# Attention and an MLP on one core: q and k stored with tokens inside, v by two pairs of heads, and the small sums one row block later

## The chip, the cores and the metric

The kernel runs on one core of a Trainium2 chip. Its engines work side by side, each on a queue of its own: TensorE multiplies matrices (PE in the profile, PEld for its weight loads), VectorE (DVE) and ScalarE (ACT) work element by element, GpSimd (POOL) adds a little, and SyncE (SP) does nothing but issue DMAs. All DMAs that SP issues stand in one queue and are issued in order. The metric is the device time of one launch in microseconds. What numpy does to the inputs ahead of the launch is not in it.

## The reference

Sigmoid attention with 8 batches, 12 heads, 448 tokens and 64 dimensions a head, and behind it an MLP over all 3,584 tokens (768 to 2,048 to 768). The weights come in 64-bit floats, the rest in 32-bit.

```python
def _attn_ref(q, k, v):                     # each (8, 12, 448, 64)
    scale = 1.0 / np.sqrt(q.shape[-1])
    scores = scale * np.matmul(q, k.transpose(0, 1, 3, 2)) - np.log(S)
    attn = 1.0 / (1.0 + np.exp(-scores))
    return np.matmul(attn, v)

def _moe_ref(x, w_in, w_out):               # x (3584, 768), w_in (768, 2048), w_out (2048, 768)
    h = x @ w_in
    g = h - np.tanh(h)
    return g @ w_out
```

## The kernel before, in words

The program goes through the batches. A batch has attention over six pairs of heads (a pair fills the 128 partitions with 2 x 64 dimensions), then a first product `moe1` (x times w_in, line 763), the function g on VectorE and ScalarE (`mix`, `halves`), and a second product `moe2` (g times w_out, lines 878 and 916). While TensorE runs `moe2` of one batch, the attention of the next is woven in step by step.

*Precision.* From batch 1 on, every 32-bit operand is scaled by a power of two and split in a high and a low float16 half, and a product takes three float16 matmuls. The scale comes from a sum of squares: `norm` squares a tile on ScalarE and adds it up (line 317), `scales` adds over the partitions by a matmul with ones (`pbn`, line 325), reads that on ScalarE (`tn`, line 327) and makes the scale from it in six small VectorE operations (`un`, `n_y`, `in`, `sn`, `rn`). These are the small sums. Batch 0 is multiplied in 32-bit and needs none.

*Layout.* A score matmul needs the 64 dimensions of a head on the partitions, but q and k lie in memory with tokens outside and dimensions inside, 256 bytes a row. `load_qk` loads a pair into `kn` and `qn`, [112 tokens, 4, 2 heads, 64]. In batch 0 `prep` turns them on TensorE (`transpose`, lines 309 and 641: into PSUM as `KT`, `QT`, then a copy to `KS` on VectorE and to `QS` on ScalarE). Later `parts` splits them in two halves `w`, and a transposing DMA on SP's queue (line 356) turns `w` into `K` and `Q`. `load_v` loads v in two to four DMAs a pair; the last 64 tokens of two pairs share a tile.

*Weights.* During batch 0's attention the 64-bit w_in is loaded in 24 pieces (`raw`, line 131, five buffers) and each is cut to 32 bits: `sta` on ScalarE (line 146), three operations on VectorE (151, 152, 155), a square (`sq`, 167 or 169) and a sum `cn`. w_out follows in 32 pieces (`rawo`, `stb`, sums `wl`). The first product of batch 0 runs in 32-bit on the cut w_in; w_in and w_out are split in halves (216, 219) in batch 0's second product.

*The order of the work.* On PE, ACT, DVE and POOL the program is issued as it is written; SP's queue is ordered by a planner in batch 0 and by the program from batch 1 on. The attention of batches 1 to 7 is a generator `stream`. For two pairs g and h = g + 1 it yields five steps: A, scores of g's first two key blocks, and products with v left over from before; B, the other scores of g, and the squares of k and q of g + 3; S, `scales(g + 2)` and the split of K of g + 2; C, scores of h, products with v, splits of Q and v of g + 2; D, the last scores of h, splits of K and Q of g + 3. When each step is issued is a table of numbers: `BLOCKS` (and `BLOCKS1` in batch 1) counts the row blocks of `moe2`, one for each of the 16 blocks of w_out's rows and each of three tiles of 128 tokens, six matmuls a block; the rest of 64 tokens counts half. In `BLOCKS` the entries are D, A, B, S, C, D, A, B, S, C, D, A, B, S, C, so S stood two blocks ahead of C: at 18, 34 and 50. Three more events at a batch's end (`batch_scales`, at the 12th entry plus 3, 5 and 7, thus at 46, 48 and 50) scale and split x for the next first product.

Of the kernel before, what the change touches and what calls it, by code (L numbers as in the profile page):

```python
# [8 lines left out]
F16 = mybir.dt.float16  # L9
BF16 = mybir.dt.bfloat16  # L10
F32 = mybir.dt.float32
# [3 lines left out]
AF = mybir.ActivationFunctionType  # L15
ALU = mybir.AluOpType
# [3 lines left out]
P = 128  # L20
D = 64
CK = 112
QT = 3
# [11 lines left out]
class Builder:  # L35
# [7 lines left out]
    BLOCKS = (8, 11, 16, 18, 20, 24, 27, 32, 34, 36, 40, 43, 48, 50, 52)  # L43
# [3 lines left out]
    BLOCKS1 = (4, 6, 7, 10, 13, 16, 18, 20, 24, 27, 32, 34, 36, 40, 43, 48, 50, 52)  # L47
# [5 lines left out]
    def __init__(self, ctx, tc, q, k, v, w_in, w_out, out):  # L53
        self.tc, self.nc = tc, tc.nc
        self.q, self.k, self.v, self.w_in, self.w_out, self.out = q, k, v, w_in, w_out, out
        self.B, self.H, self.S, _ = q.shape
        self.DM, self.DFF = w_in.shape
        self.NP = self.H // 2
# [3 lines left out]
        nc = self.nc  # L62
# [217 lines left out]
    def load_qk(self, b, j):  # L280

        out = []
        for name, src in (("kn", self.k), ("qn", self.q)):
            t = self.nat.tile([CK, 4, 2, D], F32, name=name)
            for h in range(2):
                queue = self.nc.scalar if name == "qn" and b + j == 0 else self.nc.sync
                queue.dma_start(t[:, :, h, :], src[b, 2 * j + h].rearrange("(c p) d -> p c d", c=4))
            out.append(t)
        return out

    def load_v(self, b, j, pool, tag, bufs):


        n = 2 * QT + (0 if j % 2 else 2)
        t = pool.tile([P, n, D], F32, name="vn", tag=tag, bufs=bufs)
        dma = self.nc.sync.dma_start
        for h in range(2):
            dma(t[:, h * QT : (h + 1) * QT], self.v[b, 2 * j + h, : QT * P].rearrange("(c p) d -> p c d", c=QT))
# [6 lines left out]
    def transpose(self, n, name, tag="tr", bufs=1):  # L305
        nc = self.nc
        t = self.ps.tile([P, 512], F32, name=name, tag=tag, bufs=bufs)
        for c in range(4):
            nc.tensor.transpose(t[:, c * CK : (c + 1) * CK], n[:, c].rearrange("p h d -> p (h d)"), self.ident[:CK, :CK])
        return t[:, : self.S]  # L310

    def norm(self, t, out):

        flat = t.rearrange("p a b d -> p (a b d)" if len(t.shape) == 4 else "p a d -> p (a d)")
        rows, n = flat.shape
        junk = self.sm.tile([P, 8 * D], BF16, name="sqn", tag="sq", bufs=2)
        self.nc.scalar.activation(junk[:rows, :n], flat, AF.Square, accum_out=out[:rows])  # L317
# [27 lines left out]
    def parts(self, n, s, name, act):  # L345

        nc = self.nc
        flat = n.rearrange("p c h d -> p (c h d)")
        w = self.qk.tile([CK, 2, 4 * P], F16, name="w", tag="w", bufs=2)
        if act:  # L350
            nc.scalar.activation(w[:, 0], flat, AF.Copy, scale=s[:CK])
        else:
            nc.vector.tensor_scalar(w[:, 0], flat, s[:CK], None, op0=ALU.mult)
        nc.vector.scalar_tensor_tensor(w[:, 1], flat, s[:CK], w[:, 0], op0=ALU.mult, op1=ALU.subtract)
        o = self.qk.tile([P, 2, self.S], F16, name=name, tag=name)
        nc.sync.dma_start_transpose(
            o.rearrange("p x (c t) -> p (x c) t", c=4), w.rearrange("p x e -> p (x e)")
        )
        return o
# [257 lines left out]
    def attention32(self, b, weights, rest):  # L617
# [5 lines left out]
        load = lambda j: self.load_qk(b, j) + [self.load_v(b, j, self.att, "vhl", 3)]  # L623
# [8 lines left out]

        def prep(j):
            out = []
            for n, name in ((0, "K"), (1, "Q")):
                t = self.transpose(loaded[j][n], name + "T", *((), ("mm", 2))[n])
                o = self.qk.tile([P, S], F32, name=name + "S", tag=name)
                if n:
                    nc.scalar.activation(o, t, AF.Copy)
                else:  # L640
                    nc.vector.tensor_copy(o, t)
                out.append(o[:, None])
            return out
# [17 lines left out]
        self.warm(14)  # L661
        qk = {0: prep(0)}
        self.warm(4)
        order = [(j, c) for j in range(NP) for c in (range(QT) if j % 2 else range(QT + 1))]
        for n, (j, c) in enumerate(order):
            both = (j, j + 1) if c == QT else (j,)
            ps = self.scores([qk[i][0] for i in both], [qk[i][1] for i in both], c)
# [5 lines left out]
            if c == (1, 0)[j % 2] and j + 1 < NP:  # L673
                qk[j + 1] = prep(j + 1)
# [398 lines left out]
```

## Time and profile before

| | us |
|---|---|
| median of 3 runs | 1241.29 (1240.48 to 1241.41) |
| the profiled execution, own time | 1240.89 |
| its span | 1239.1 |
| PE busy | 1182.8 (95%) |
| DVE busy | 927.8 (75%) |
| ACT busy | 887.6 (72%) |
| POOL busy | 77.7 (6%) |
| loads of k and q | 96 and 96 DMAs of 112 KB |
| loads of v | 96 DMAs of 96 KB, 48 of 32 KB |
| transposing DMAs | 42 for K, 42 for Q |
| DMA packets under 512 bytes | 213,936 of 225,679 |

A stage has its own bound, and the shares above are averages over all stages. A timeline row reads: start, length, engine, line, operation, output and inputs, and in brackets the idle time ahead of it with what ended it. A row of waits reads: who waited, for whom, microseconds in total, how often, the longest. A row of a group of instructions reads: count, then busy time in total and the mean in ns of one, then the idle time ahead of the group. SPq stands for the issue of a DMA on SP's queue.

### The profile page before, as it was taken

The numbers are of one execution on the slowest core, as the hardware profiler recorded it, in microseconds if no ns is written. First come the engines' busy times: TensorE is split into PE (matmuls) and PEld (weight loads), VectorE is DVE, ScalarE is ACT, GpSimd is POOL, SyncE is SP. The second block draws the span as 40 slices with busy tenths as digits, with TensorE's granted clock in tenths as the row PEclk, the third lists the DMA queues.
The fourth block names the chain that finished last, engine by engine and source line by source line (L and its number), as shares of the span: only waits on it lengthen the run. The fifth ranks groups of instructions, "written<-read, shape, count | busy, mean of one in ns | idle before, by whom it ended". The sixth has DMA issues, their size and how long they took to land.

```text
span 1239.1 us, 19719 instructions
## 1 busy us (share of the span) xinstructions
PE 1182.8 (95%) x7633; PEld 606.5 (49%) x7633; DVE 927.8 (75%) x1376; ACT 887.6 (72%) x1238; POOL 77.7 (6%) x62
## 2 busy tenths in 40 slices
PE   8889867899999999999999999999999999999998
PEld 3235423455445555555555555455554555455555
DVE  5899967788976789667976789667976789636930
ACT  5767776877887678876887678875887768754820
POOL 0100000000002000200002000110001000110000
PEclk9999988899999999999999999999999999999999
DMA  9973358230045400542014410442014510300000
GB/s 228 264 206 91 83 115 213 56 75 7 1 88 116 94 17 1 114 92 65 1 44 102 91 35 1 100 106 65 1 43 88 96 44 1 65 22 20 2 13 33
DMA packets 225679, 89.78 MB, mean 72 GB/s; under 512 B 213936, under 2 KB 215728, under 8 KB 225584
## 3 DMA queue, kind: packets, MB, share of 16 engines
q1 hardware_dynamic: 224656, 88.28, 30.6%
q8 instruction: 60, 0.98, 0.3%
q10 hardware_dynamic: 928, 0.23, 0.1%
q14 instruction: 35, 0.29, 0.1%
HBM read 58.20 MB, written 11.01 MB: 56 GB/s over the span
## 4 chain that ended last, share of the span: by engine, by line
PE 77%; DVE 8%; ACT 8%; issue 3%; DMA 3%; SPq 1%; ACTq 0%; DVEq 0%
PE ph L763 30%; PE po L878 27%; PE acc L411 8%; PE sc L380 7%; PE por L916 4%; ACT a L391 3%; ACT sqn L317 2%; DMA raw<-moe_w_in 1%; DMA qn<-q 1%; DVE m L837 1%; DVE m L848 1%; DVE sta L152 1%; DVE m L851 1%; DVE m L844 1%; DVE g L748 1%
## 5 line engine op out<-in xcount | busy, mean ns | idle before, releaser
L878 PE MATMUL po<-wo,g 128*128 128x384 f16 x2304 | 397.4, 328 | 6.2 <-ACT wo L216 3.1
L763 PE MATMUL ph<-xhl,wi 128*128 128x448 f16 x2016 | 382.6, 352 | 0.0
L878 PEld LDWEIGHTS <-g 128*128 128x128 f16 x2304 | 220.2, 99 | 176.5 <-issue 38.4
L763 PEld LDWEIGHTS <-wi 128*128 128x128 f16 x2016 | 196.7, 98 | 185.0 <-issue 1.8
L398 DVE SCALAR_TENSOR_TENSOR ahl<-a,ahl 128x896 f16<-128x896 f32 x126 | 156.6, 1277 | 140.9 <-ACT ahl L397 140.5
L391 ACT ACTIVATE a<-sc,nls,rn 128x896 f32<-128x896 f32 x147 | 156.1, 1088 | 61.9 <-PE sc L380 59.0
L833 ACT ACTIVATE u<-ph,ih 128x896 f32<-128x896 f32 x64 | 64.4, 1006 | 94.3 <-PE ph L763 89.7
L397 ACT ACTIVATE ahl<-a 128x896 f16<-128x896 f32 x126 | 113.1, 940 | 0.6
L380 PE MATMUL sc<-Q,K 64*128 64x448 f16 x1008 | 106.3, 368 | 4.7 <-ACT a L391 2.5
L837 DVE SCALAR_TENSOR_TENSOR m<-ph,ihk,u 128x896 f32<-128x896 f32 x64 | 73.6, 1150 | 35.0 <-ACT th L835 34.6
L747 ACT ACTIVATE g<-m,Sg 128x896 f16<-128x896 f32 x64 | 66.6, 1041 | 34.4 <-DVE m L851 29.1
L851 DVE COPY_PREDICATED m<-u,th 128x896 f32<-128x896 uint32 x64 | 77.4, 1210 | 6.6
L411 PE MATMUL acc<-ahl,vhl 128*64 128x448 f16 (+1 forms) x864 | 81.0, 357 | 0.0
L748 DVE SCALAR_TENSOR_TENSOR g<-m,Sg,g 128x896 f16<-128x896 f32 x64 | 73.5, 1148 | 8.1 <-ACT g L747 8.1
L848 DVE SCALAR_TENSOR_TENSOR m<-q,m 128x896 f32<-128x896 f32 x64 | 69.9, 1092 | 10.9 <-ACT q L847 3.8
L793 PE MATMUL ph<-x,wi 128*128 128x448 f32 x192 | 75.1, 540 | 0.2 <-DVE x L423 0.2
L838 DVE SCALAR_TENSOR_TENSOR th<-ph,ih,th 128x896 f32<-128x896 f32 x64 | 73.3, 1146 | 0.0
L850 ACT ACTIVATE u<-u,b 128x896 f32<-128x896 f32 x64 | 66.7, 1043 | 7.2 <-DVE m L837 5.2
L439 POOL TENSOR_TENSOR x<-x 128x448 f32<-128x448 f32 x24 | 22.4, 932 | 786.3 <-ACT x L427 786.3
L380 PEld LDWEIGHTS <-K 64*128 64x128 f16 x1008 | 36.7, 99 | 68.9 <-issue 45.6
L844 DVE SCALAR_TENSOR_TENSOR m<-q,m 128x896 f32<-128x896 f32 x64 | 69.6, 1088 | 0.0
L916 PE MATMUL por<-wo,g 128*64 128x384 f16 x768 | 65.8, 327 | 1.1 <-ACT o L907 1.1
(133 smaller groups left out, 1195.0 us busy)
## 6 DMA issues: line engine op xcount, KB each, us to landing
raw<-moe_w_in SPq DMA_DIRECT2D x24, 512.0 KB, 5.2
rawo<-moe_w_out SPq DMA_DIRECT2D x32, 384.0 KB, 4.4
kn<-k SPq DMA_DIRECT2D x96, 112.0 KB, 3.0
qn<-q SPq DMA_DIRECT2D x94, 112.0 KB, 3.1
vn<-v SPq DMA_DIRECT2D x96, 96.0 KB, 2.9
out<-o SPq DMA_DIRECT2D x21, 384.0 KB, 2.4
vn<-v SPq DMA_DIRECT2D x48, 32.0 KB, 2.4
out<-orem SPq DMA_DIRECT2D x16, 96.0 KB, 2.2
```

What stands on the lines that cost most here:

```text
L380: self.nc.tensor.matmul(ps[i * m : (i + 1) * m, h, : self.S], K[i][r, w, c * P : c * P + m], Q[i][r, x, :], start=(n == 0), stop=(n == len ...
L391: self.nc.scalar.activation(a[:, 0], ps[:, :, : self.S], AF.Sigmoid, bias=self.nls, scale=scale)
L397: nc.scalar.activation(A[:, 0], a[:, 0], AF.Copy, scale=A_SCALE)
L398: nc.vector.scalar_tensor_tensor(A[:, 1], a[:, 0], A_SCALE, A[:, 0], op0=ALU.mult, op1=ALU.subtract)
L411: self.nc.tensor.matmul(acc[i][h * D : (h + 1) * D, : self.S], v[k, w, 2 * QT + h if half else h * QT + c], A[k, x, h], start=(n == 0 and ...
L748: nc.vector.scalar_tensor_tensor(g[:, 1], m, Sg, g[:, 0], op0=ALU.mult, op1=ALU.subtract)
L763: nc.tensor.matmul(ph[:, e, :S], self.wi[:, c * self.NB + k, part, e * P : (e + 1) * P], xhl[c][:, x, :], start=(i == 0), stop=(i == 3 * s ...
L837: V.scalar_tensor_tensor(m, ps, ihk, u, op0=ALU.mult, op1=ALU.mult)
L848: V.scalar_tensor_tensor(m, q2, C2, m, op0=ALU.add, op1=ALU.mult)
L851: V.copy_predicated(m, u.bitcast(U32), th)
L878: nc.tensor.matmul(po[i][:, :H], gs[f // 2][:, x, f % 2, tk * P : (tk + 1) * P], self.wo[:, i * self.NF + f, w], start=(f == 0 and n == 0) ...
L916: nc.tensor.matmul(po[e * D : (e + 1) * D, :H], gs[f // 2][:, x, f % 2, nm:S], self.wo[:, e * self.NF + f, w], start=(f == 0 and n == 0), ...
```

## The change

numpy lays q and k out as [batch, pair, 128, 448] with tokens inside, and v as [batch, two pairs, 128, 14, 64], so that each tile is one DMA of whole rows: 1,792 bytes a partition for k and q, 2,048 or 1,536 for v. `transpose` and `prep` are gone: batch 0 multiplies the loaded tiles, those of odd pairs being loaded into the buffers `K` and `Q`. `parts` writes the halves straight into `K` and `Q`; the buffer `w` and the transposing DMAs are gone. The squares of w_in, half of which lay in `w`'s buffers, get four of their own. The four warm-up matmuls behind the first transposes join the 14 ahead of them. In the tables step S moves from 18, 34 and 50 to 19, 35 and 51; in `BLOCKS0` and at the first S of `BLOCKS1` (at 6) it stays.

```diff
-    BLOCKS = (8, 11, 16, 18, 20, 24, 27, 32, 34, 36, 40, 43, 48, 50, 52)
+    BLOCKS = (8, 11, 16, 19, 20, 24, 27, 32, 35, 36, 40, 43, 48, 51, 52)
-    BLOCKS1 = (4, 6, 7, 10, 13, 16, 18, 20, 24, 27, 32, 34, 36, 40, 43, 48, 50, 52)
+    BLOCKS1 = (4, 6, 7, 10, 13, 16, 19, 20, 24, 27, 32, 35, 36, 40, 43, 48, 51, 52)
...
-        pool, tag = (self.qk, "w") if k % 2 else (self.sm, "sq")
-        p["sq"] = pool.tile([P, p["piece"][3]], BF16, name="sq", tag=tag, bufs=2)
+        p["sq"] = self.sm.tile([P, p["piece"][3]], BF16, name="sq", tag="sq", bufs=4)
...
-    def load_qk(self, b, j):
+    def load_qk(self, b, j, tags=("kn", "qn")):
         out = []
-        for name, src in (("kn", self.k), ("qn", self.q)):
-            t = self.nat.tile([CK, 4, 2, D], F32, name=name)
-            for h in range(2):
-                queue = self.nc.scalar if name == "qn" and b + j == 0 else self.nc.sync
-                queue.dma_start(t[:, :, h, :], src[b, 2 * j + h].rearrange("(c p) d -> p c d", c=4))
+        for tag, src in zip(tags, (self.k, self.q)):
+            pool = self.nat if tag in ("kn", "qn") else self.qk
+            t = pool.tile([P, self.S], F32, name=tag + "n", tag=tag, bufs=2)
+            queue = self.nc.scalar if src is self.q and b + j == 0 else self.nc.sync
+            queue.dma_start(t, src[b, j])
             out.append(t)
...
     def load_v(self, b, j, pool, tag, bufs):
+        at = 0 if j % 2 == 0 else 2 * QT + 2
         n = 2 * QT + (0 if j % 2 else 2)
         t = pool.tile([P, n, D], F32, name="vn", tag=tag, bufs=bufs)
-        dma = self.nc.sync.dma_start
-        for h in range(2):
-            dma(t[:, h * QT : (h + 1) * QT], self.v[b, 2 * j + h, : QT * P].rearrange("(c p) d -> p c d", c=QT))
-        if j % 2 == 0:
-            for i in range(2):
-                src = self.v[b, 2 * (j + i) : 2 * (j + i) + 2, QT * P :]
-                dma(t[i * D : (i + 1) * D, 2 * QT :], src.rearrange("h t d -> t h d"))
+        self.nc.sync.dma_start(t, self.v[b, j // 2, :, at : at + n])
...
     def parts(self, n, s, name, act):
-        flat = n.rearrange("p c h d -> p (c h d)")
-        w = self.qk.tile([CK, 2, 4 * P], F16, name="w", tag="w", bufs=2)
+        o = self.qk.tile([P, 2, self.S], F16, name=name, tag=name)
         if act:
-            nc.scalar.activation(w[:, 0], flat, AF.Copy, scale=s[:CK])
+            nc.scalar.activation(o[:, 0], n, AF.Copy, scale=s)
         else:
-            nc.vector.tensor_scalar(w[:, 0], flat, s[:CK], None, op0=ALU.mult)
-        nc.vector.scalar_tensor_tensor(w[:, 1], flat, s[:CK], w[:, 0], op0=ALU.mult, op1=ALU.subtract)
-        o = self.qk.tile([P, 2, self.S], F16, name=name, tag=name)
-        nc.sync.dma_start_transpose(
-            o.rearrange("p x (c t) -> p (x c) t", c=4), w.rearrange("p x e -> p (x e)")
-        )
+            nc.vector.tensor_scalar(o[:, 0], n, s, None, op0=ALU.mult)
+        nc.vector.scalar_tensor_tensor(o[:, 1], n, s, o[:, 0], op0=ALU.mult, op1=ALU.subtract)
...
-        load = lambda j: self.load_qk(b, j) + [self.load_v(b, j, self.att, "vhl", 3)]
+        load = lambda j: self.load_qk(b, j, (("kn", "qn"), ("K", "Q"))[j % 2]) + [self.load_v(b, j, self.att, "vhl", 3)]
...
-        self.warm(14)
-        qk = {0: prep(0)}
-        self.warm(4)
+        self.warm(18)
...
-            ps = self.scores([qk[i][0] for i in both], [qk[i][1] for i in both], c)
+            ps = self.scores([loaded[i][0][:, None] for i in both], [loaded[i][1][:, None] for i in both], c)
...
-            if c == (1, 0)[j % 2] and j + 1 < NP:
-                qk[j + 1] = prep(j + 1)
```

The lines of the changed program have other numbers. On ScalarE at the start of batch 0, before (`a` is a sigmoid, `QS` the copy of the turned q, `sta` the first step on a piece of w_in):

```order
L626 ACTIVATE one<-nls 128x1
L639 ACTIVATE QS<-QT 128x448
L391 ACTIVATE a_184<-sc,nls 128x896
L391 ACTIVATE a_196<-sc,nls 128x896
L639 ACTIVATE QS<-QT 128x448
L146 ACTIVATE sta<-raw 128x512
```

And now:

```order
L606 ACTIVATE one<-nls 128x1
L371 ACTIVATE a_161<-sc,nls 128x896
L371 ACTIVATE a_173<-sc,nls 128x896
L144 ACTIVATE sta<-raw 128x512
L371 ACTIVATE a_193<-sc,nls 128x896
```

Both copies of Q ahead of the first piece of w_in are gone; the two sigmoids ahead of it stay.

On SP's queue in batch 0's second product, from the first store of `oh` back, before (`rawo` are pieces of w_out):

```order
L131 DMA rawo<-moe_w_out 128x384 x3
L871 DMA out<-oh 128x384
L356 DMA_TRANSPOSE K<-w 128x8x112
L287 DMA kn<-k 112x4x64 x2
L131 DMA rawo<-moe_w_out 128x384
L356 DMA_TRANSPOSE Q<-w 128x8x112
L298 DMA vn<-v 128x3x64 x2
L287 DMA qn<-q 112x4x64 x2
L131 DMA rawo<-moe_w_out 128x384 x5
```

And now:

```order
L129 DMA rawo<-moe_w_out 128x384 x6
L835 DMA out<-oh 128x384
L284 DMA knn<-k 128x448
L129 DMA rawo<-moe_w_out 128x384
L284 DMA qnn<-q 128x448
L294 DMA vn<-v 128x384
L129 DMA rawo<-moe_w_out 128x384 x5
```

Two transposes and half of the loads' issues are gone from between the pieces of w_out, which keep their order among themselves.

On TensorE in batch 1's second product, around the first moved S, before (`po0` and `po1` are the two halves of a row of outputs, each `g` serves two row blocks):

```order
L878 LDWEIGHTS g_2566
L878 MATMUL po1_3347<-wo_95,g_2566 128x384
L325 MATMUL pbn_3360<-ss1_114,onesf_90 128x6
L878 LDWEIGHTS g_2636
L878 MATMUL po0_3346<-wo_95,g_2636 128x384
```

And now:

```order
L842 MATMUL po1_3150<-wo_95,g_2385 128x384
L842 LDWEIGHTS g_2455
L842 MATMUL po0_3149<-wo_95,g_2455 128x384
...
L842 MATMUL po1_3150<-wo_95,g_2455 128x384
L310 MATMUL pbn_3169<-ss1_114,onesf_90 128x6
```

The sum `pbn` stood where one `g` gives way to the next, and stands now six matmuls later, in the middle of the next `g`.

More of the change, by code (lines that the diff above doesn't have):

```diff
@@ L21 @@
 D = 64
-CK = 112
 QT = 3
@@ L55, in __init__ @@
         self.q, self.k, self.v, self.w_in, self.w_out, self.out = q, k, v, w_in, w_out, out
-        self.B, self.H, self.S, _ = q.shape
+        self.B, self.NP, _, self.S = q.shape
         self.DM, self.DFF = w_in.shape
-        self.NP = self.H // 2
         self.NC = self.DM // P
@@ L631, in attention32 @@
         accs = {}
[L633 to L643, printed above, removed]
         def open_acc(j):
@@ L1066 @@
     }
-    shape = (q.shape[0] * q.shape[2], q.shape[1] * q.shape[3])
+    shape = (B * S, H * D)
     args["out"] = nc.dram_tensor("out", shape, F32, kind="ExternalOutput").ap()
```

25 lines of the change are left out of this document (12 added, 13 removed).

## The prediction

> **What bounds the kernel now.** I read busy time by stage first (the stages are cut where the chain of waits changes its lines), then each engine's waits, then the timeline where TensorE stands still. The columns are the stretch, its length, busy time and count of PE, PEld, DVE, ACT and POOL, the granted clock, the DMA share and GB/s.
>
> ```profile
> 0.00:76.40 76.40, 65.12 (x305) 21.78 (x306) 55.02 (x101) 52.81 (x82) 6.10 (x10) 0.98 0.99 251
> 76.40:157.70 81.30, 73.63 (x216) 36.48 (x215) 76.90 (x128) 56.99 (x78) 0.00 (x0) 0.98 0.38 97
> 157.70:197.00 39.30, 27.04 (x154) 9.91 (x153) 29.01 (x56) 30.14 (x52) 1.14 (x1) 0.89 0.58 139
> 197.00:278.00 81.00, 74.52 (x497) 37.30 (x496) 61.98 (x143) 60.43 (x123) 3.42 (x3) 0.94 0.45 108
> 428.00:568.70 140.70, 138.76 (x969) 72.89 (x969) 108.88 (x151) 107.89 (x148) 11.18 (x8) 1.00 0.27 60
> ```
>
> Four regimes. Batch 0's attention (to 76.4 us) has its DMA engines 99% busy. Batch 0's first product (to 157.7) has VectorE 76.90 us of 81.30. The transition (to 278) has TensorE idle for 39.30 - 27.04 = 12.3 and 81.00 - 74.52 = 6.5 us, at a reduced clock. A later batch (here batch 2) is TensorE's: 138.76 of 140.70. The change touches all four, so each gets its own term.
>
> **Term A, batch 0's attention.** DMA rates first (a stretch of 256-byte rows of k and q; then one of w_in, 4 KB a row), then the conversion of w_in, whose end releases the product.
>
> ```profile
> 498.00:499.00 1.00, 1.00 (x8) 0.59 (x6) 0.00 (x0) 1.00 (x3) 0.05 (x1) 1.00 1.02 193
> 51.00:54.00 3.00, 3.00 (x22) 1.45 (x20) 2.20 (x4) 2.80 (x5) 0.00 (x0) 1.00 0.98 366
> ```
>
> ```profile
> 6.09 0.55 PE L309 MATMUL KT<-ident,kn 112*128 112x112 f32 x4
> 6.47 0.55 PE L309 MATMUL QT<-ident,qn 112*128 112x112 f32 x4
> 10.81 1.01 ACT L391 ACTIVATE a<-sc,nls 128x896 f32<-128x896 f32 x1 [0.91 <-PE sc L380]
> 13.88 0.66 ACT L146 ACTIVATE sta<-raw 128x512 f32<-128x512 f32 x1
> 14.57 0.43 DVE L151 TENSOR_SCALAR sta<-sta 128x512 uint32<-128x512 uint32 x1 [1.78 <-ACT sta L146]
> 74.10 0.69 DVE L155 SCALAR_TENSOR_TENSOR wi<-raw,sta 128x512 uint32<-128x512 uint32 x1
> ```
>
> ```profile
> L641 DVE COPY KS<-KT 128x448 f32<-128x448 f32 x6 | 3.7, 618 | 10.2 <-PE KT L309 10.2
> ```
>
> ```profile
> ACT sta L146 <- DMA raw<-moe_w_in: 5.2, 2, 2.7
> ```
>
> VectorE works on w_in's 24 pieces from 14.57 to 74.10 + 0.69 = 74.8, which is 60.2 us. Its busy time in the stage is 55.02, of which the first K copy (0.6) lies ahead of 14.57; add the 5.2 us for which ScalarE, one step ahead of it, waited for raw w_in, and 59.6 of the 60.2 are told. So VectorE is the bound of this stage, and a DMA share of 99% costs it only about 5.2 us.
>
> The change takes 5 K copies (3.1 us) out of this stretch, and whole rows should take the 5.2 away: q, k and v of batch 0 are 3 x 12 x 448 x 64 x 4 B = 4.13 MB, 21.4 us of DMA at 193 GB/s and 11.3 at 366. The new rows are 1,792, 2,048 and 1,536 bytes long. The trace has none of that size, so their rate lies between the two, and I take one near the upper: a row is then much nearer to one packet of 4 KB than to seven of 256 B. VectorE needs 60.2 - 3.1 - 5.2 = 51.9 us. It also starts earlier. The first piece on ScalarE comes behind the second sigmoid (10.81 + 0.9 = 11.7), the copy of Q and the transposes that this copy waits for (13.88); these go, and the sigmoids move up by some 0.8 us, since one set of transposes (6.09 to 7.02) stood ahead of the first scores, while the four warm matmuls that stood there too are only put ahead of their old place. ScalarE begins near 10.9, VectorE 0.7 later, near 11.6. End: 11.6 + 51.9 = 63.5 in place of 74.8, a gain of 11.3. ScalarE, 52.81 busy here less six Q copies, is nearly as full, and the two wait for each other in turn, so I take 10. Ends: 6.1 if the 5.2 of waiting stay, 13 if the stage closes tighter than now.
>
> **Term B, the first product.** VectorE's chain sets the pace (76.90 of 81.30), and of it only the splits of K and Q shrink, from 512 columns to 448.
>
> ```profile
> L354 DVE SCALAR_TENSOR_TENSOR w<-kn,sn,w 112x512 f16<-112x512 f32 x42 | 31.6, 752 | 6.6 <-ACT w L351 5.3
> ```
>
> Four of them lie here; an eighth of 752 ns is 94 ns at most, 0 at least: 0.3 us. The same shortening in the later batches lies beside a full TensorE (138.76 of 140.70) and gives nothing. Two more edits cost nothing: the squares of w_in keep four buffers in all, two of them only change their pool, and numpy's laying out of q, k and v happens before the launch.
>
> **Term C, the transition.** TensorE's gaps that go back to a DMA:
>
> ```profile
> 176.28 0.63 ACT L317 ACTIVATE sqn<-kn 112x512 bf16<-112x512 f32 x1 [1.06 <-DMA kn<-k]
> 178.99 0.63 ACT L317 ACTIVATE sqn<-qn 112x512 bf16<-112x512 f32 x1 [1.99 <-DMA qn<-q]
> 180.27 0.32 PE L878 MATMUL po<-wo,g 128*128 128x384 f16 x1 [2.71 <-ACT wo L216]
> ...
> 211.62 0.56 ACT L146 ACTIVATE stb<-rawo 128x384 f32<-128x384 f32 x1 [3.29 <-DMA rawo<-moe_w_out]
> 216.14 0.33 PE L179 MATMUL wl<-stb,onesb 128*128 128x384 bf16 x1 [3.25 <-DVE stb L152]
> ```
>
> ```profile
> 199.63 1.28 SPq L356 DMA_TRANSPOSE K<-w  x1
> 200.96 1.12 SPq L287 DMA_DIRECT2D kn<-k  x2
> ...
> 203.19 1.22 SPq L356 DMA_TRANSPOSE Q<-w  x1
> 204.51 1.66 SPq L298 DMA_DIRECT2D vn<-v  x2
> 206.22 1.34 SPq L287 DMA_DIRECT2D qn<-q  x2
> 207.60 2.79 SPq L131 DMA_DIRECT2D rawo<-moe_w_out  x5
> ```
>
> ScalarE's norms wait 1.06 + 1.99 = 3.05 for k and q, whose issue stood behind two transposes; the w_out split behind them holds TensorE for 2.71. SP's queue issues from 199.63 to 207.60 almost without a break, and the five w_out pieces at its end arrive 3.29 late for ScalarE, which holds TensorE for 3.25. Without the two transposes (1.28 + 1.22) and half of the other six issues (4.1 / 2) the pieces leave some 4.5 us earlier, unless v's slot holds the queue. I take both gaps as gone: 2.7 + 3.25. Below that end lies zero, if the next wait takes the place of each; above it a knock-on through the clock:
>
> ```profile
> 341.76 0.39 PE L325 MATMUL pbn<-ss,onesf 128*128 128x6 f32 x2 [1.88 <-ACT sqn L317]
> 344.00:346.00 2.00, 2.00 (x14) 0.63 (x12) 1.97 (x4) 1.57 (x3) 0.00 (x0) 0.50 0.00 0
> 218.00:220.00 2.00, 2.00 (x8) 0.53 (x6) 1.90 (x6) 2.00 (x3) 0.00 (x0) 0.50 0.77 180
> ```
>
> After a gap of 1.88 us the granted clock is 0.50, and behind the gap at 216 it is 0.50 again. A row of 2 us at half clock loses 1.0 us, and the stretch reaches beyond its row on one side or both, so I price one at 1.7 (between 1.0 and 2.0) and take one as gone. Ends: 0, or two of them, 3.4.
> The Trainium skill ("TensorE: Matmul & The Clock Gate", The HAM clock gate) has the clock halved after a whole idle window of about 3.4 us. The halving agrees with the trace, but here 1.88 us was enough; by the page alone neither 2.71 nor 3.25 would trip it, and the sum would be 1.7 smaller, 1215.3.
>
> **Term D, the later batches.** TensorE's 140.70 - 138.76 = 1.94 us of idle time in a batch lie at the small sums, one of three waits being that at 506.17 (its neighbours in the program stand around it, the two rows ahead are from the transition):
>
> ```profile
> 195.28 0.39 PE L325 MATMUL pbn<-ss,onesf 128*128 128x4 f32 x2 [2.70 <-ACT sqn L317]
> 233.09 0.39 PE L325 MATMUL pbn<-ss,onesf 128*128 128x6 f32 x2 [3.23 <-ACT sqn L317]
> 505.93 0.19 ACT L317 ACTIVATION_READ_ACCUMULATOR sqn<-qn 112x1 f32 x1
> 506.17 0.39 PE L325 MATMUL pbn<-ss,onesf 128*128 128x6 f32 x2 [0.65 <-ACT sqn L317]
> 506.42 2.11 PE L878 MATMUL po<-wo,g 128*128 128x384 f16 x12
> 507.70 0.25 ACT L327 ACTIVATE tn<-pbn,tiny 128x6 f32<-128x6 f32 x1
> 516.23 0.74 PE L380 MATMUL sc<-Q,K 64*128 64x448 f16 x6
> 517.82 0.48 DVE L353 TENSOR_SCALAR w<-kn,sn 112x512 f16<-112x512 f32 x1
> ```
>
> ```profile
> PE pbn L325 <- ACT sqn L317: 17.5, 18, 3.2
> ```
>
> ScalarE's last norm ends at 506.12, TensorE is free at 506.17 - 0.65 = 505.52. One row block of `moe2` (six matmuls, half of 2.11: about 1.0 us) put ahead brings the sum to 506.5: the wait is covered by products that had to run anyway, with 0.4 us to spare. `tn`, the next reader, starts at 507.70 behind two splits on ScalarE, so it isn't later. The step issues `pbn`, `tn`, six small VectorE operations and K's split; its only DMA, the transpose, is gone, so it passes nothing on SP's or GpSimd's queue. The 18 waits are 17.5 us; the three at steps that keep their place take 2.70, 3.23 and 1.88 (341.76, above); 9.7 remain, all at moved steps. I take 9.7 (ends 0, if ScalarE turns out to be later with it, and 9.9). At a batch's end the step also passes VectorE's last two splits of x, which then come some 2 us earlier, ahead of the product that needs them; the split of K and Q behind them has until the next batch's first scores.
>
> **The sum.** 10 + 0.3 + 2.7 + 3.25 + 1.7 + 9.7 = 27.6. The profiled execution took 1240.9 (span 1239.1 and 1.8 around it), so 1213.2; the median of the runs is 0.4 above it: 1213.6.
>
> **The rivals.** First, slow rows: 1,792 bytes move no faster than 256, ScalarE's 5.2 us stay, A is 6.1 and the time 1217.5. For it: no such row in the trace; against: four kilobytes reach 366. Second, the transition gives its gaps back: C is 0, 1221.2. For it: VectorE and ScalarE are both in the chain there, and a wait at 233 for ScalarE follows at once; against: those engines stand idle too while they wait for the DMA. Third, D fails: the sums stay late or the split waits, 1223.3. Against it: 0.4 us of room. Fourth, more than I count: the transition's other half-clock stretch and further waits go as well, some 7 us more: 1206.6.
> On the other side: the splits now write K and Q themselves, where a buffer and a transpose lay between. VectorE must wait until TensorE has read the old K, and holds up the split of the weights queued behind it. Of K that is read until 516.23 + 0.74 = 517.0 the split starts at 517.82, 0.85 later. If in each of the 18 pairs of heads the wait ended on TensorE with more than 27.6 / 18 = 1.5 us, the kernel would be slower; with 2.5 us each it takes 1213.6 + 45 = 1258.6. The 0.85 of room speaks against it.
>
> **Chances and range.** Forecast 0.52, slow rows 0.12, transition given back 0.18, D fails 0.06, more gain 0.08, slower 0.04, of which 0.01 lies near zero. The measurement tells 0.2% (2.5 us) from no change. Faster 0.96, same 0.01, slower 0.03. The range reaches from the fourth rival, with A's upper end, to the third with some of the first: 1204 to 1226.
>
> **What would show it.** A: `wi`'s last piece ends near 64 us and ScalarE's wait for `moe_w_in` is gone. C: no wait for `kn` or `qn` at the norms, `wl` no longer waits 3 us, fewer slices of reduced clock. D: the wait of `pbn` for `sqn` falls from 17.5 to about 8 and a later batch takes 138.8 us. Wrong if VectorE waits for TensorE before the splits of K, or if the first stage ends past 69 us.

## The result and the profile after

The changed kernel takes 1211.51 us (median of 4 runs, 1210.02 to 1212.40), the kernel before 1240.88 beside it: ratio 0.9763, 95% interval 0.9746 to 0.9780. The profiled execution took 1212.4 (span 1210.6), which is 28.5 less than the one of before.

Busy time by stage of the kernel after, cut where its own chain changes stage (columns as in the prediction):

```profile
0.00:66.90 66.90, 57.34 (x257) 16.67 (x258) 51.76 (x95) 50.05 (x76) 5.65 (x10) 1.00 0.84 294
66.90:148.00 81.10, 73.51 (x218) 36.55 (x218) 76.75 (x128) 56.54 (x78) 0.00 (x0) 0.99 0.28 80
148.00:189.00 41.00, 31.18 (x176) 11.42 (x177) 31.31 (x64) 31.61 (x56) 1.14 (x1) 0.85 0.44 140
189.00:262.30 73.30, 69.19 (x475) 35.76 (x472) 59.90 (x134) 58.20 (x122) 3.61 (x3) 0.95 0.25 78
410.40:548.50 138.10, 138.10 (x969) 72.92 (x969) 108.73 (x151) 107.11 (x147) 11.97 (x8) 1.00 0.14 41
```

The first stage is 9.5 us shorter and its DMA share is down from 0.99 to 0.84. In the transition (third and fourth row) TensorE stands still for 9.8 + 4.1 = 13.9 us in place of 12.26 + 6.48 = 18.7. A later batch has no idle time on TensorE at all.

The first stage on the timeline after: the first sigmoid, VectorE's first and last piece of w_in.

```profile
8.94 1.01 ACT L371 ACTIVATE a<-sc,nls 128x896 f32<-128x896 f32 x1 [6.27 <-PE sc L360]
12.46 0.43 DVE L149 TENSOR_SCALAR sta<-sta 128x512 uint32<-128x512 uint32 x1 [11.16 <-ACT sta L144]
64.58 0.69 DVE L153 SCALAR_TENSOR_TENSOR wi<-raw,sta 128x512 uint32<-128x512 uint32 x1
```

A small sum of a later batch, on TensorE after (with its neighbours) and before (the row ahead of the wait shown in the prediction):

```profile
485.80 3.10 PE L842 MATMUL po<-wo,g 128*128 128x384 f16 x18
488.73 0.28 PE L310 MATMUL pbn<-ss,onesf 128*128 128x6 f32 x2
488.87 1.14 PE L842 MATMUL po<-wo,g 128*128 128x384 f16 x6
```

```profile
503.40 2.12 PE L878 MATMUL po<-wo,g 128*128 128x384 f16 x12
```

Before, the next product began 506.42 - (503.40 + 2.12) = 0.90 behind the end of the last; after, it begins as the last one ends (488.87 against 485.80 + 3.10 = 488.90). A moved sum was thus worth about 0.9, of which the row of the wait showed 0.65; the other 0.25 lie between the sum's start (506.17) and the next product's.

The waits after that answer to those of before, and the granted clock of the two pages (before, then after; 40 slices). For `wl` the row of before has 9.1 us in 8 waits, the longest 3.3.

```profile
PE pbn L310 <- ACT sqn L302: 8.2, 3, 3.8
PE wl L176 <- DVE stb L150: 7.2, 8, 1.4
ACT stb L144 <- DMA rawo<-moe_w_out: 3.9, 3, 2.8
ACT Q L335 <- DVE sn L321: 24.7, 6, 4.6
```

```profile
PEclk9999988899999999999999999999999999999999
```

```profile
PEclk9999999899999999999999999999999999999999
```

The dates of the stages come from the chain of waits: where the chain enters batch 0's first product, and the first products of batches 1, 2 and 3. The rows of after, to show how the table below is made (66.90; 262.31 - 66.90 = 195.4; 410.36 - 262.31 = 148.05; 548.53 - 410.36 = 138.17):

```profile
66.90 4.51 PE ph L757 x12
262.31 47.79 PE ph L727 x252
410.36 54.59 PE ph L727 x288
548.53 54.59 PE ph L727 x288
```

| kernel | first stage | to batch 1 | batch 1 | a later batch | median us |
|---|---|---|---|---|---|
| before | 76.4 | 201.5 | 150.0 | 140.7 | 1240.9 to 1242.0 |
| after | 66.9 | 195.4 | 148.05 | 138.17 | 1211.5 |
| e1 tables alone | 75.1 | 201.6 | 148.2 | 138.16 | 1230.2 |
| e2 layout alone | 66.7 | 194.8 | 149.6 | 140.39 | 1220.4 |
| e3 short rows | 68.0 | 193.2 | 146.6 | 138.16 | 1212.3 |
| e4 14 warm | 65.6 | 195.1 | 146.6 | 138.17 | 1209.4 |
| e5 filled gaps | 67.4 | 191.7 | 146.7 | 138.16 | 1207.6 |
| e7 copies | 68.3 | 193.7 | 148.05 | 138.17 | 1211.4 |
| e8 two issues | 70.9 | 193.7 | 146.6 | 138.16 | 1213.4 |
| e9 transposes | 67.4 | 197.2 | 146.6 | 138.16 | 1212.0 |
| e10 10 warm | 65.0 | 193.5 | 148.15 | 138.16 | 1208.5 |
| e11 e4 and e5 | 65.1 | 192.0 | 146.75 | 138.16 | 1205.9 |
| e12 old traffic | 75.8 | 200.6 | 148.2 | 138.17 | 1225.3 |

The stages are those of one profiled execution each. "To batch 1" is batch 0's first product and the transition together, and is what the experiments below call the transition when they give its length; e6's chain does not pass through these products, so it has no row. The scatter shows in kernels whose program is the same in a stage: after, e2, e5 and e9 end the first one at 66.7 to 67.4, and after, e2, e4, e7 and e10 take 193.5 to 195.4 to batch 1. With the new tables batch 1 is near 148.1 or near 146.6 (see the last section). One of e2's six executions took 2415.7 us; its ratio leaves that one out, and its median would be 1220.21 without it. e1's profiled execution (1226.7) was the fastest of its six, e2's (1222.9) the slowest of the other five.

### The profile page after: what moved, and what is told of

Read it like the earlier page. It is cut to its first block, busy times and chain, and to the rows that moved or that the text cites. A ratio compares the mean times of both kernels' runs of the same rounds, so it can differ in the third digit from the quotient of the medians.

```text
span 1210.6 us, 19076 instructions
## 1 busy us (share of the span) xinstructions
PE 1170.5 (97%) x7585; PEld 602.1 (50%) x7585; DVE 923.0 (76%) x1370; ACT 878.8 (73%) x1232; POOL 81.4 (7%) x62
## 3 DMA queue, kind: packets, MB, share of 16 engines
q1 hardware_dynamic: 33824, 68.99, 18.1%
## 4 chain that ended last, share of the span: by engine, by line
PE 81%; DVE 11%; ACT 4%; issue 3%; DMA 1%; DVEq 0%; ACTq 0%; SPq 0%
PE ph L727 31%; PE po L842 29%; PE sc L360 7%; PE acc L391 7%; PE por L880 5%; DVE sta L150 1%; DVE stb L150 1%; ACT a L371 1%; DVE m L801 1%; DVE wi L153 1%; DVE sta L149 1%; PE warm L89 1%; DVE stb L149 1%; DVE m L812 1%; ACT sqn L302 1%
## 5 line engine op out<-in xcount | busy, mean ns | idle before, releaser
L378 DVE SCALAR_TENSOR_TENSOR ahl<-a,ahl 128x896 f16<-128x896 f32 x126 | 160.6, 1309 | 135.4 <-ACT ahl L377 135.3
L711 ACT ACTIVATE g<-m,Sg 128x896 f16<-128x896 f32 x64 | 66.6, 1041 | 35.0 <-DVE m L815 29.4
L419 POOL TENSOR_TENSOR x<-x 128x448 f32<-128x448 f32 x24 | 26.4, 1100 | 770.2 <-ACT x L407 770.2
L757 PE MATMUL ph<-x,wi 128*128 128x448 f32 x192 | 75.1, 540 | 0.2 <-DVE x L403 0.2
L802 DVE SCALAR_TENSOR_TENSOR th<-ph,ih,th 128x896 f32<-128x896 f32 x64 | 73.3, 1145 | 0.0
L814 ACT ACTIVATE u<-u,b 128x896 f32<-128x896 f32 x64 | 66.7, 1043 | 7.4 <-DVE m L801 5.5
## 6 DMA issues: line engine op xcount, KB each, us to landing
vn<-v SPq DMA_DIRECT2D x24, 192.0 KB, 2.4
```

Source lines behind the costliest of these rows:

```text
L378: nc.vector.scalar_tensor_tensor(A[:, 1], a[:, 0], A_SCALE, A[:, 0], op0=ALU.mult, op1=ALU.subtract)
L757: nc.tensor.matmul(ph[:, e, :S], self.where("in", c)[:, f * P : (f + 1) * P], xs[c], start=(c == 0), stop=(c == self.NC - 1),)
```

## The experiments

**e1, the tables alone.**

```diff
 (the kernel before)
-    BLOCKS = (8, 11, 16, 18, 20, 24, 27, 32, 34, 36, 40, 43, 48, 50, 52)
+    BLOCKS = (8, 11, 16, 19, 20, 24, 27, 32, 35, 36, 40, 43, 48, 51, 52)
 (and the same three entries of BLOCKS1)
```

> The kernel before with the new tables alone (small sums one row block later), q, k and v as they were, transposes kept. Own theory: the tables are the whole gain of the later batches, and each of the 15 moved sums was worth its 0.65 us wait plus about 0.2 us in which TensorE fills and drains around the gap, 0.85 in all: 15 x 0.85 = 12.7, so about 1228.2 us, a later batch takes 138.2 and pbn waits for sqn about 8 us in all. By the term as predicted (0.65 each, 9.7): 1231.2. Rival: the sums need the shorter norms of the new layout, or the transpose of K that goes with the step now holds SP's queue: 1235 to 1241, with pbn waits left in every batch.

Measured: 1230.16 (ratio 0.9910, 0.9895 to 0.9924), between the 1228.2 of the first theory and the 1231.2 of the term as predicted; the profile tells which. By its list of waits `pbn` waits 7.8 us, 3 times, and by its chain a batch is 563.07 - 424.91 = 138.16:

```profile
PE pbn L325 <- ACT sqn L317: 7.8, 3, 3.2
```

```profile
424.91 54.59 PE ph L763 x288
563.07 54.59 PE ph L763 x288
```

From batch 1's product to the end the profiled runs of before, e1 and after take 961.1, 948.3 and 948.3. The tables by themselves are the whole gain of the later batches; neither the shorter norms nor the missing transposes are needed for it. 961.1 - 948.3 = 12.8 over 15 moved sums is 0.85 each.

**e2, the layout alone.** The diff is e1's turned round, in the changed kernel.

> The changed kernel with the old tables: the layout alone. Own theory: layout and tables act in different stages and add up, so what the tables gave (12.7) is given back: 1211.5 + 12.7 = 1224.2, a later batch takes 140.7 and pbn waits near 18 us again, while the first stage still ends near 66.7. Rival: the layout is worth part of the later batches' gain, since the norms are 448 columns in place of 512 and no transpose is left: 1217 to 1221, with a later batch at 139 to 140.

Measured: 1220.35 (0.9827, 0.9815 to 0.9840), below the 1224.2 of the first theory and in the range of the rival. The first stage and the transition are those of after, and the waits are back, in the list of waits and on TensorE's timeline:

```profile
PE pbn L310 <- ACT sqn L302: 16.5, 18, 4.0
```

```profile
489.23 0.39 PE L310 MATMUL pbn<-ss,onesf 128*128 128x6 f32 x2 [0.54 <-ACT sqn L302]
```

Norms of 448 columns shorten each wait by 0.1, which is 0.3 a batch (140.39): the rival's mechanism, at less than half of its size. By the medians the two halves of the change give 11.8 and 21.7, together 29.4, so some 4 us are counted twice (3 by the ratios). Of these 1.6 are the shorter waits (batch 1's product to the end takes 959.5, before 961.1), which the tables remove anyway; the rest is not told from the scatter of the runs.

**e3, short rows.**

```diff
-            queue.dma_start(t, src[b, j])
+            queue.dma_start(t.rearrange("p (c t) -> p c t", t=D), src[b, j].rearrange("c p t -> p c t"))
 (numpy lays k, q and v out in chunks of 64 elements; v likewise)
```

> The changed kernel with q, k and v laid out by numpy in chunks of 64 elements, so that each DMA moves rows of 256 bytes (896 for a pair of heads of k, as before); the tiles on the chip, the operations and the number of DMAs are those of the changed kernel. Own theory: the length of the rows is worth the 5.2 us that ScalarE waited for w_in in the first stage, and in the transition part of the gap of 3.25: 5 to 8 us, so 1216.5 to 1219.5, with the first stage's end 5 us later and its DMA share back near 0.99. Rival one: the transposes, the copies and the number of DMAs did it all, the bytes in flight are hidden: 1211.5 to 1212.5. Rival two: short rows hold up SP's queue too, in every stage: above 1222.

Measured: 1212.29 (0.9762, 0.9749 to 0.9776). Against after this is no difference that can be told. The rows are short (132,912 packets under 512 bytes), the DMA share of the first stage is back at 1.02, and ScalarE waits for w_in half as long as before, but the stage ends only 1.1 later, little more than the scatter. From the page, the windows (DMA share second to last) and the waits:

```profile
DMA packets 144649, 70.43 MB, mean 58 GB/s; under 512 B 132912, under 2 KB 134704, under 8 KB 144560
```

```profile
0.00:68.00 68.00, 58.40 (x257) 17.00 (x258) 52.09 (x95) 49.93 (x76) 5.48 (x10) 0.97 1.02 287
```

```profile
ACT sta L145 <- DMA raw<-moe_w_in: 2.5, 2, 1.7
```

Own theory fell: the length of the rows alone is not what was won.

**e4, 14 warm matmuls** in place of 18 (`self.warm(18)` to `self.warm(14)`).

> The changed kernel with 14 warm matmuls ahead of the first scores in place of 18, since the first sigmoid did not move up (8.94 us, before 8.88): the four added warm matmuls fill the place of the transposes. Own theory: the first scores start about 1.2 us earlier (four warm matmuls take 1.04), k and q having landed by then, and the whole first stage with them, since VectorE is its bound: about 1 us less, 1210.5, first sigmoid near 7.8. Rival one: k and q land later than that, the scores wait for the DMA: 1211.5. Rival two: fewer warm matmuls leave the clock reduced in the first stage: 1212 to 1214.

Measured: 1209.43 (0.9741, 0.9728 to 0.9754). The first scores run at 6.53 in place of 7.87, and the stage ends 1.3 earlier. The rest of the 2.1 lies within the two lengths of batch 1 (148.05 and 146.6). The added warm matmuls had taken the place of the transposes.

**e5, filled gaps.**

```diff
+        for _ in range(self.fills.pop(0) if self.fills else 0):
+            nc.tensor.matmul(pb, self.onesb, self.onesb[:, None, :].to_broadcast([P, 4, P]), start=True, stop=True)
...
+        if self.fill:
+            self.warm(self.fill.pop(0))
...
+        self.fill, self.fills = [], [0, 0, 11, 17, 7]
...
+        self.fill = [0, 10, 10]
```

`fill` puts 10 extra warm matmuls ahead of each of two scores that wait, `fills` 11, 17 and 7 ahead of the `pbn` that wait, into the same PSUM tile.

> The changed kernel with idle work on TensorE: extra warm matmuls whose result nobody reads, put where TensorE stands still in the transition and in batch 1 (10 ahead of each of the two scores that wait 2.3 us near 145 and 148, 11, 17 and 7 ahead of the three pbn that wait 2.59, 3.82 and 1.80 us). They are sized to end before the wait does, so the waits for the other engines stay. Own theory: the gaps trip the clock, and the half-clock stretches behind them (about 2.5, 2.8, 2.5 and 1.1 us lost, from the granted clock by window) go; where VectorE and ScalarE are full, part of it is not regained: 4 to 9 us less, 1202.5 to 1207.5, and the granted clock is 1.00 from 148 to 262. Rival one: the clock falls for another reason or the other engines set the pace behind the gaps: 1210.5 to 1212.5. Rival two: the extra matmuls stand in the way: 1213 to 1216.

Measured: 1207.58 (0.9725, 0.9712 to 0.9739), 3.9 below after, at the upper end of the first theory. The granted clock is full in nearly all of the transition, and of the wait of 3.82 only 0.15 is left behind the filler (windows, then TensorE's timeline):

```profile
148.00:189.00 41.00, 32.95 (x209) 13.04 (x208) 33.49 (x69) 34.45 (x61) 1.14 (x1) 0.96 0.46 147
189.00:259.00 70.00, 67.35 (x472) 35.38 (x470) 57.26 (x129) 54.52 (x115) 3.53 (x3) 1.00 0.24 77
```

```profile
210.34 3.83 PE L311 MATMUL pbn<-onesb 128*128 128x512 bf16 x17
214.32 0.39 PE L313 MATMUL pbn<-ss,onesf 128*128 128x6 f32 x2 [0.15 <-ACT sqn L302]
```

So the half clock comes from TensorE's own gaps and costs time, but less than half of the 9 to 10 us that the clock loses there comes back (3.7 against after's transition, some 2 against those of e7 and e10): VectorE and ScalarE are nearly full beside it, and new waits for ScalarE appear (1.40 for `tn`, 0.94 for a norm).

**e6, the other sums later too.**

```diff
-    BLOCKS0 = (2, 5, 7, 8, 12, 16, 20, 22, 24, 31, 38)
-    BLOCKS1 = (4, 6, 7, 10, ...)
+    BLOCKS0 = (2, 5, 8, 8, 12, 16, 20, 26, 26, 31, 38)
+    BLOCKS1 = (4, 8, 8, 10, ...)
```

> The changed kernel with the three small sums that kept their place moved too: in batch 0 from row block 7 to 8 and from 22 to 26 (with the scores behind it from 24 to 26), in batch 1 from 6 to 8 (with the scores behind it from 7 to 8). Own theory: the waits of pbn that are left, 2.59, 3.82 and 1.80 us, fall to about 1.5, 0 and 0, and with them the half clock behind the last two: 6.7 + 3.6 = 10 us at the most, of which VectorE and ScalarE, nearly full there, give back up to half: 1202 to 1206.5. Rival: the scores of the next pair of heads come later and with them the splits behind; the wait only changes its place: 1210.5 to 1214.

Measured: 1211.98 (0.9764, 0.9749 to 0.9779): nothing won. Batch 1's first product begins at 262.77 on TensorE's timeline (after 262.25), which shows why:

```profile
213.48 0.39 PE L310 MATMUL pbn<-ss,onesf 128*128 128x6 f32 x2
213.80 1.31 PE L360 MATMUL sc<-Q,K 64*128 64x448 f16 x12
222.96 5.49 PE L391 MATMUL acc<-a,vn 128*64 128x448 f32 x20 [7.85 <-ACT tn L312]
```

`pbn` waits no more, but the products with v now wait 7.85 for `tn`: `acc` takes over the PSUM buffer that `tn` reads, and on ScalarE 12 splits of w_out and 7 of w_in stand between the last norm (213.24) and `tn` (222.65), since the step was moved behind them too. The wait only changed its place, as the rival said, though not to the next pair's scores but into the very step that was moved.

**e7, the copies of K and Q put back.**

```diff
+                if n:
+                    nc.scalar.activation(o, loaded[j][n], AF.Copy)
+                else:
+                    nc.vector.tensor_copy(o, loaded[j][n])
```

> The changed kernel with the copies of K (VectorE) and Q (ScalarE) of batch 0 put back, one of each per pair of heads, as plain copies from the loaded tile; no transposes, whole rows. Own theory: VectorE is the bound of the first stage, so its 6 x 0.62 = 3.7 us of copies come back, the first of them ahead of its first piece with little cost, 3.1 to 4: 1214.6 to 1215.5, first stage ending near 70.5. Rival one: both copies count, VectorE's 3.7 and ScalarE's 6 x 0.54 = 3.2, since the two engines wait for each other: 1218.4. Rival two: the copies were hidden beside the waits for w_in: 1211.5 to 1212.5.

Measured: 1211.35 (0.9757, 0.9744 to 0.9770). In the run profiled the first stage ends 1.4 later (a copy from the loaded tile takes 0.39 on VectorE, from PSUM it took 0.62), and the total shows nothing.

**e8, two DMAs for each load** (64 partitions each).

```diff
-            queue.dma_start(t, src[b, j])
+            for h in range(2):
+                queue.dma_start(t[h * D : (h + 1) * D], src[b, j][h * D : (h + 1) * D])
 (v likewise)
```

> The changed kernel with each load of k, q and v issued as two DMAs of 64 partitions each, the same bytes in rows of the same length; twice as many issues for them on SP's queue, as before. Own theory: the number of issues is a small part: in the first stage some 36 issues more at 0.4 us put w_in's pieces later by up to the 2 or 3 us that neither the copies, nor the rows, nor the earlier start explain; in the transition 6 more ahead of w_out's pieces: 1212.5 to 1215. Rival one: SP's queue has room everywhere and the issues cost nothing: 1210.5 to 1212. Rival two: they are all that was won in the transition: 1217 and more, with TensorE waiting over 3 us for the w_out sums.

Measured: 1213.43 (0.9775, 0.9761 to 0.9788), within the first theory's range. The first stage is 4.0 longer, and ScalarE's list of waits has 3.9 for w_in; the way to batch 1 is not longer (193.7).

```profile
ACT sta L144 <- DMA raw<-moe_w_in: 3.9, 3, 3.0
```

**e9, DMA transposes put back** on SP's queue, into a tile that nobody reads.

```diff
+        junk = self.qk.tile([P, 7, 112], F16, name="junk", tag="junk", bufs=2)
+        nc.sync.dma_start_transpose(junk, o[:112].rearrange("p x e -> p (x e)"))
```

> The changed kernel with a DMA transpose behind each split of K and Q on SP's queue, as before the change, but into a tile that nobody reads (112 rows of 896 columns, seven blocks of 112); loads, splits and tables are those of the changed kernel. Short rows, copies and twice the issues each left the transition (from batch 0's second half product to batch 1's product) at 193 to 194 us, against 201.5 before and 195.4 after, so by elimination the transposes are its cause. Own theory: they come back on SP's queue ahead of k, q and w_out's pieces, the norms wait for k and q again and the w_out split or wl holds TensorE: the transition takes 198 to 201, the time is 1214.5 to 1217.5; the later batches stay at 138.2. Rival: what the transition won is that nobody waits for the transposes' results and that the splits are shorter; transposes into nothing cost under 1 us: 1210.5 to 1212.5.

Measured: 1212.00 (0.9759, 0.9736 to 0.9781). The transition (197.2) is 1.8 longer than after's, the longest of the five with the same program, and a wait of 2.41 for the w_out sums is back, but the total is the rival's.

**e12, all the old traffic at once**: e3's rows, e8's issues (for v two or four, as before) and e9's transposes in one kernel. They are not the very DMAs of before: k and q come in halves of 64 partitions, and a transpose has seven blocks where it had eight.

> The changed kernel with the DMA traffic of the kernel before, all of it at once: rows of 256 bytes, two issues for each load of k and q and two or four for v, and a DMA transpose behind each split of K and Q (into a tile that nobody reads). What is left of the change: no transposes on TensorE, no copies of K and Q in batch 0, splits of 448 columns that write K and Q themselves, the new tables. Short rows alone cost 0.8 us against the changed kernel, double issues alone 1.9, transposes alone 0.5: 3.2 in all, each too little to hold an engine for long. Own theory: they share one queue and its engines, so together they use up the room that each alone left: the first stage ends 5 to 7 us later than after, with ScalarE waiting about 5 us for w_in, and the transition takes 199 to 201.5 with a wait of 2 us or more for k, q or w_out on TensorE's side: 1220 to 1224. Rival: the costs add up as they stand: 1214 to 1216; then most of what the transition won (201.5 to about 194) is the shorter splits on VectorE and ScalarE.

Measured: 1225.29 (0.9870, 0.9854 to 0.9887), 1.3 above the range of the first theory and far above the rival's. The first stage ends at 75.8, which is 8.9 later than after and not 5 to 7, and the transition takes 200.6: nearly the 76.4 and 201.5 of before. In the first stage VectorE begins its pieces at 11.46, earlier than after, and has no copies to make, yet its last piece starts at 73.43; in the transition the norms wait for k and q, and TensorE for the w_out sums (timelines of VectorE, ScalarE and TensorE, then a row of the waits):

```profile
11.46 0.43 DVE L150 TENSOR_SCALAR sta<-sta 128x512 uint32<-128x512 uint32 x1 [10.16 <-ACT sta L145]
73.43 0.69 DVE L154 SCALAR_TENSOR_TENSOR wi<-raw,sta 128x512 uint32<-128x512 uint32 x1
...
174.87 0.58 ACT L312 ACTIVATE sqn<-knn 128x448 bf16<-128x448 f32 x1 [1.41 <-DMA knn<-k]
176.22 0.58 ACT L312 ACTIVATE sqn<-qnn 128x448 bf16<-128x448 f32 x1 [0.68 <-DMA qnn<-q]
183.97 0.33 PE L177 MATMUL wl<-stb,onesb 128*128 128x384 bf16 x1 [2.69 <-DVE stb L151]
214.84 0.33 PE L177 MATMUL wl<-stb,onesb 128*128 128x384 bf16 x1 [2.42 <-DVE stb L151]
```

```profile
ACT sta L145 <- DMA raw<-moe_w_in: 7.2, 3, 4.4
```

One by one the three cost 0.8, 1.9 and 0.5 us, together 13.8. (v's third and fourth issue are in none of the single runs.) So the medians make a chain: 1242.0 before, less 11.8 for the tables (e1) is 1230.2, less 4.9 for the transposes on TensorE, the copies and the longer splits is 1225.3 (e12), less 13.8 for the traffic is 1211.5. The middle link is the weakest: the profiled spans of e1 and e12 (1225.0 and 1224.7) do not show it.

**e10, 10 warm matmuls.**

> The changed kernel with 10 warm matmuls ahead of the first scores in place of 18. With 14 the first scores came at 6.5 in place of 7.87 and the first stage ended 1.3 us earlier; the first k had landed by about 4.4. Own theory: four fewer give as much again, if q has landed by 5.2 too: 1208 to 1208.5. Rival one: q's landing or w_in's first piece (issued at 1.65, some 6 us to land) is what ends last now: as with 14, 1209.4. Rival two: TensorE stands still before its scores and the clock falls: 1210 to 1213.

Measured: 1208.52 (0.9731, 0.9708 to 0.9754), 0.9 below e4, but the two intervals overlap. The first scores now run partly slower, 1.42 us for four in place of 1.02, and the stage ends 0.5 earlier than with 14: the second rival's mechanism takes back part of the gain. On TensorE's timeline:

```profile
5.57 1.42 PE L360 MATMUL sc<-qnn,knn 64*128 64x448 f32 x4
```

**e11, e4 and e5 together.**

> The changed kernel with both what filled the gaps (7.58 in the thousand and two hundred, 3.9 less than the changed kernel) and 14 warm matmuls in place of 18 (2.1 less in the median, 1.3 by the end of the first stage). Own theory: different stages, they add up: 1205.5 to 1206.3. Rival: what 14 warm matmuls gain is lost again in the transition, where VectorE and ScalarE are full: 1207.5.

Measured: 1205.89 (0.9709, 0.9687 to 0.9731). They add up, and this kernel is 5.6 us faster than the changed one, the best of this study.

## Why the prediction was right, and where not

The forecast of 1213.6 lies 2.1 above the measured 1211.5. The sum of 27.6 came out as 28.5 in the profiled executions, but its terms shifted, and that the whole agrees so well is in part luck: A has the right size for a wrong reason, and what D was too small (3.1) makes up for what B and C were too large in this execution (1.9).

*A, 10 worked out, 9.5 measured (76.4 to 66.9): right in size, wrong in its reason.* The step that failed is the reading that VectorE is the bound of the first stage and the full DMA engines cost it "only about 5.2 us". e12 takes away the copies and starts VectorE 3.1 earlier, as the sum counted, and with the old traffic the stage still ends at 75.8: these two pieces, 6.1 in the sum, give 0.6. VectorE's time from the start of its first piece to the end of its last, before, in e12 and after (busy time of VectorE is the third one):

```profile
14.57:74.79 60.22, 51.62 (x247) 15.91 (x244) 52.88 (x86) 46.12 (x71) 5.40 (x4) 0.97 1.00 260
11.46:74.12 62.66, 50.38 (x217) 13.58 (x216) 51.42 (x82) 44.30 (x67) 4.77 (x4) 0.92 1.04 266
12.46:65.27 52.81, 45.22 (x217) 12.35 (x216) 50.85 (x82) 44.45 (x67) 4.95 (x4) 1.00 0.85 301
```

It stands idle for 7.3 us before, 11.2 in e12 and 2.0 after. (The prediction took the busy time of the whole stage, 55.02, of which only 52.88 lie in this stretch, and so told nearly all of the 60.2.) What was taken off VectorE came back as waiting. The stage has two limits: with the old traffic the DMAs end it near 76, with the new one VectorE ends it near 67, and A is the distance between them, not a sum of pieces taken off VectorE. The rule that row length is the cause failed as well: 256-byte rows cost 1.1 (e3), twice the issues 4.0 (e8), both together 8.9 (e12). The first rival (slow rows) priced a rate that does not improve; the rate did improve, but what mattered was how much room the rows and issues leave each other. The rate of 193 GB/s was also misread: the traffic from 498 to 499 is mostly Q's transpose (issued at 496.57; the loads of k were issued from 497.85 on, and their traffic begins past 499.1). With no transposes the short rows of k and q moved 263 GB/s at a DMA share of 1.18 (e3, 492.10 to 493.60), and whole rows 362 at 0.98 (after, 494.95 to 495.95). The sum did not use the 193.

A's start was 0.9 off, 12.46 for 11.6. I had the first sigmoid move up by 0.8 because the four warm matmuls "are only put ahead of their old place". In a row the 18 take 6.75 us (from 1.19), where 14 and 4 had taken 5.06 and 1.03, so they fill the transposes' place too: the scores start at 7.87 (before 7.82) and the sigmoid stays at 8.94 (before 8.88). With four fewer (e4) the scores start 1.3 earlier, and so does the stage's end.

*B and C, 7.95 worked out, 6.1 measured (201.5 to 195.4), and 6.4 to 8.0 in the other four kernels with the same transition (193.5 to 195.1).* The gaps went as said: no wait for kn or qn at the norms, and the wait of 3.25 for the w_out sums is down to 0.29, though its cause is not gone; ScalarE still waits 2.83 for one piece, and TensorE has work ahead to cover it. All the waits for these sums fell less, from 9.1 to 7.2, since a new one of 1.44 came. Of 5.95 us of gaps 4.8 came back (18.7 to 13.9 of idle time). The 1.7 for the clock did not come in the profiled execution: 1 - clock times length is 0.11 x 39.3 + 0.06 x 81 = 9.2 us before and 0.15 x 41 + 0.05 x 73.3 = 9.8 after. The gap of 3.82 at a small sum that stays put halves the clock as the old ones did (0.50 from 217.20 to 221.20). In the same two stretches of e2, e4, e7 and e10 the same sum gives 6.8 to 7.6, some 2 below before, so the term is not refuted either: the draw from run to run is as large as the term. That SP's queue and its DMAs were the cause of the gaps is shown by all of the old traffic together (e12, 200.6, with the waits for k, q and the w_out sums back); the transposes alone (e9, 197.2) return 1.8 of it, hardly beyond the scatter, short rows or double issues alone nothing.

*D, 9.7 worked out, 12.8 measured.* Right mechanism, mis-sized term: I took the wait's 0.65 for the whole price of a gap. Behind a wait the 0.25 from the sum's start to the next product's are lost too; without one they pass beside the products around the sum. So a moved sum is worth 0.85 and not 0.65. e1 shows it without the layout. `pbn` fell to 8.2 as said, and a later batch takes 138.17 rather than 138.8.

*The rivals.* The transition did not give its gaps back. The slower rival, splits that wait for TensorE to have read the old K and Q, has no row: the splits wait for `sn`, their own sum (24.7 us in 6 waits on ScalarE, 17.1 before), which is the moved step being later, beside a TensorE that is busy all the time.

## What to carry to other kernels

A stage with full DMA engines and a nearly full compute engine has two limits, and a sum of waits cannot tell which one binds: taking the smaller load off alone may give nothing (e12: 0.6 for 6.1), and each part of the old traffic put back alone cost 0.5 to 1.9 us of 13.8. Price a gap on an engine that works in order by the distance between the work ahead and behind, not by the wait that the row shows. When a step is moved past a wait, look at everything the step issues: on the queue of the other engine it also moves behind whatever stood between (e6).

## What the runs showed of the hardware

The same gap does not always cost the clock. Ahead of batch 1's first small sum TensorE stands still for 1.78 to 1.91 us in eleven of these kernels. In six of them (before, after, e1, e2, e7, e10) the clock of the next 6 us is 0.72, in the other five (e3, e4, e8, e9, e12) 1.00. With the new tables batch 1 takes 148.05 to 148.16 in the first case and 146.6 in the second; only e12, at 148.24 with the full clock, stands out, since there TensorE also waits 0.54, 0.92 and 0.29 near 360 to 365. After, and e4:

```profile
326.02 0.39 PE L310 MATMUL pbn<-ss,onesf 128*128 128x6 f32 x2 [1.80 <-ACT sqn L302]
326.52:332.52 6.00, 6.00 (x48) 2.47 (x46) 5.54 (x13) 4.85 (x7) 0.00 (x0) 0.72 0.01 3
```

```profile
324.36 0.39 PE L310 MATMUL pbn<-ss,onesf 128*128 128x6 f32 x2 [1.78 <-ACT sqn L302]
324.86:330.86 6.00, 5.86 (x56) 3.06 (x54) 5.55 (x13) 5.00 (x8) 0.00 (x0) 1.00 0.01 3
```

The longest of the eleven, 1.91 in e12, kept the clock, and one of the shortest, 1.78 in e2, lost it, so length does not decide it. The Trainium skill ("TensorE: Matmul & The Clock Gate", The HAM clock gate) has the activity judged in a window that runs free of the kernel; the draw agrees with that, while its whole idle window of about 3.4 us does not agree with gaps of 1.8.

Short rows cost DMA time all the same: e3 moves the same 68.99 MB in 21.6% of the 16 engines' span, after in 18.1%. The rows in question carry 33 MB of it; if all bytes of after cost the same, their share grew by roughly 40%, an estimate. The transposes alone take more: e9 has 25.3%, for no more time lost. Both stayed hidden, as 1.02 of DMA share in the first stage did. What in short rows and double issues together exceeds the room, the engines or SP's queue, was not told apart.
